# Global queries' scores: 128 weight columns instead of 32, and the global keys repeated behind the last key block

## The chip, the core and the metric

The kernel runs on one core of a Trainium2 chip. The metric is the time of one execution on the device in microseconds (us). Three runs of the kernel before took 1181.5, 1179.32 and 1181.81 us; their median is 1181.5 us.

## The reference, cut to what matters

```python
def _attn_ref(q_l, k_l, v_l, q_g, k_g, v_g):          # 8 batches, 8 heads, 512 local and 32 global tokens, 64 wide
    k_all = np.concatenate([k_g, k_l], axis=2)
    v_all = np.concatenate([v_g, v_l], axis=2)
    s_g = scale * np.matmul(q_g, k_all.transpose(0, 1, 3, 2))      # global queries see all 544 keys
    out_g = np.matmul(sm(s_g), v_all)
    s_ll = scale * np.matmul(q_l, k_l.transpose(0, 1, 3, 2))
    s_ll = np.where(mask, s_ll, -1000000000.0)                     # mask: abs(pos[:, None] - pos[None, :]) <= 32
    s_lg = scale * np.matmul(q_l, k_g.transpose(0, 1, 3, 2))
    s_l = np.concatenate([s_lg, s_ll], axis=-1)                    # local queries: 32 global keys and a window
    out_l = np.matmul(sm(s_l), np.concatenate([v_g, v_l], axis=2))
    return np.concatenate([out_g, out_l], axis=2)

def _moe_ref(x, w_gate, w_val, w_out):                # 4608 tokens, 512 wide, 1536 hidden
    gate = 1.0 / (1.0 + np.exp(-(x @ w_gate)))
    val = x @ w_val
    return (gate * val @ w_out).astype(np.float32)
```

The attention output, heads side by side, is the input x of the gated network. All data are float32.

## The kernel before, in words

**Layout.** For each batch and head the host writes one array with 64 rows (the width of a head): 256 local queries, then the extended keys, then the other 256 local queries, then the 32 global queries. The extended keys are four blocks of 160 columns behind 32 zero columns; block j holds 64 local keys, the 32 global keys, and the next 64 local keys. 32 zero columns end them, which makes 704 (`KEXT`). So the global keys already stand once in each block, between the two halves of its local keys.

**Two forms of attention.** Fifty-two heads take a split form: each float32 operand is cast to a rounded part (`qk_hi`, a cast on ScalarE, L197) and a remainder (`kl` and part of `qk_hi`, subtractions on GpSimd, L198 and L200), and each score product is made twice, once per part, over 128 rows. The first twelve heads (all of batch 0, whose 512 tokens are worked on in two half chunks, and four of batch 1) take a native float32 form over 64 rows, in which every such product is two passes in the trace.

**Attention of local queries** (`local_unit`): two query blocks at a time, L234 (scores into PSUM), L248 and L251 (softmax on VectorE and ScalarE), L254 to L218 (normalising into `p_buf`), L270 (transposes on TensorE), L281 and L282 (the transposed weights into SBUF as `pt`: a cast on ScalarE, then a subtraction on VectorE), L301 and L302 (products with the values), L304 to L306.

**Global queries** (`global_scores`, once per head). The weights of the product are the 32 global queries; the moving operand is the extended keys. One bank, `sa` (named `bank_x`), takes two products of 256 columns per part (L318): the first 64 columns of each of the four blocks, then the last 64 of each. A second bank, `sb` (named `bank_y`), takes the 32 global keys (L320). ScalarE copies both banks into 32 rows of `pg` (L322, L323). When four heads have filled the 128 rows, `global_group` makes the softmax over columns 0 to 543 and the products with the values.

**The gated network** (`ffn_stream`): for each chunk of 512 tokens and each of 12 tiles of the hidden width, 12 products of 512 columns for the gate (`bank_g`, L400), 12 for the value (`bank_v`, L400), and 12 of the output (`bank_o`, L437) for the tile before.

**What sets the order.** A queue of events with written due times places the attention's pieces between groups of four network products. A scheduler then orders each engine's instructions by priority and allots buffers. All attention banks and `bank_g` and `bank_v` share four PSUM buffers (tag `att`), so a product that opens a bank waits until the readers of the bank that had the buffer are done. In the first 160 us the network's weights are also loaded and converted: L137 and L141 on ScalarE, L139 and L140 on VectorE, L142 on GpSimd, loads by L126.

## Time and profile before

| | |
|---|---|
| median of 3 runs | 1181.5 us (1179.32 to 1181.81) |
| the profiled execution | 1179.81 us, of which the span from first to last instruction is 1177.9 us |
| TensorE products (PE) | busy 1146.4 us, 97% of the span |
| TensorE weight loads (PEld) | busy 962.3 us, 82% |
| VectorE (DVE), ScalarE (ACT), GpSimd (POOL) | 773.7 us, 753.2 us, 413.3 us |
| granted TensorE clock | 1.000 |

Products are pipelined: the duration of one includes its way through the array, so 0.28 us for 256 columns does not mean that the next one starts 0.28 us later. What a product costs its engine is the distance between starts, and that is read from the timeline. An idle time is printed behind the instruction that ended it, with the instruction it waited for.

### The profile page before, as it was taken

Reading aid. Unit: us, or ns where it says so; the run is one execution under the profiler, and the core shown is the slowest. Engines: PE = TensorE matmul, PEld = TensorE weight load, DVE = VectorE, ACT = ScalarE, POOL = GpSimd, SP = SyncE. Lnnn points to the kernel's source line nnn. Section 1 sums busy time; section 2 is a strip of 40 time slices with the busy share of each in tenths; the row PEclk is TensorE's granted clock in tenths of the full one; section 3 lists DMA queues with packets and bytes.
Section 4 is the critical chain, followed back from the end, with each engine's and each line's share of the span. In section 5 each row is a group of like instructions: output and inputs, shape, how many; then the busy total and the mean of one; then the engine's idle time right before and its main releaser. Section 6 shows DMA issues by size and latency. Waiting matters only on the chain.

```text
span 1177.9 us, 19115 instructions
## 1 busy us (share of the span) xinstructions
PE 1146.4 (97%) x6596; PEld 962.3 (82%) x6596; DVE 773.7 (66%) x2132; ACT 753.2 (64%) x1737; POOL 413.3 (35%) x408
## 2 busy tenths in 40 slices
PE   8999999999999999999999999999999999999998
PEld 7777788888888888888888888888888888888897
DVE  5677657577676677667676677667676677533343
ACT  5898877566675676666675676666675675532343
POOL 2444435334353444334352444334452443100000
PEclk9999999999999999999999999999999999999999
DMA  8888844333443343343343343343344342122143
GB/s 295 283 288 279 259 134 128 95 116 94 115 116 113 106 115 98 106 140 90 113 115 114 105 116 98 107 149 91 103 116 122 99 118 81 44 100 72 54 151 118
DMA packets 59489, 151.81 MB, mean 129 GB/s; under 512 B 6144, under 2 KB 19456, under 8 KB 59392
## 3 DMA queue, kind: packets, MB, share of 16 engines
q1 hardware_dynamic: 59392, 150.59, 42.2%
q8 instruction: 52, 0.85, 0.3%
q14 instruction: 45, 0.37, 0.1%
HBM read 135.36 MB, written 15.20 MB: 128 GB/s over the span
## 4 chain that ended last, share of the span: by engine, by line
PE 75%; DVE 11%; ACT 8%; issue 3%; DMA 2%; POOL 1%; SPq 0%; ACTq 0%; DVEq 0%; POOLq 0%
PE bank_v L400 20%; PE bank_g L400 19%; PE bank_o L437 19%; PE bank_x L234 4%; DVE p_buf L218 4%; PE bank_y L270 4%; ACT s_sb L251 3%; PE bank_x L301 2%; PE bank_x L302 2%; PE bank_x L318 2%; PE bank_x L361 1%; DVE bank_v L420 1%; DVE bank_v L421 1%; PE bank_o L110 1%; ACT hh L423 1%
## 5 line engine op out<-in xcount | busy, mean ns | idle before, releaser
L400 PE MATMUL bank_v<-xt,wv 128*128 128x512 f32 (+1 forms) x1440 | 328.3, 364 | 14.1 <-DVE pt L282 14.1
L400 PE MATMUL bank_g<-xt,wg 128*128 128x512 f32 (+1 forms) x1440 | 330.4, 364 | 0.1
L437 PE MATMUL bank_o<-wo,hh 128*128 128x512 f32 x1224 | 329.2, 400 | 1.2 <-ACT hh L423 1.2
L400 PEld LDWEIGHTS bank_v<-xt,wv 128*128 128x128 f32 x1440 | 237.1, 189 | 51.0 <-issue 16.0
L400 PEld LDWEIGHTS bank_g<-xt,wg 128*128 128x128 f32 x1440 | 236.8, 189 | 37.4 <-issue 2.5
L437 PEld LDWEIGHTS bank_o<-wo,hh 128*128 128x128 f32 x1224 | 217.2, 189 | 41.8 <-ACT hh L423 3.0
L251 ACT ACTIVATE s_sb<-s_sb,nm 128x192 f32<-128x192 f32 (+1 forms) x240 | 110.4, 462 | 98.2 <-DVE nm L248 97.3
L218 DVE TENSOR_SCALAR p_buf<-s_sb,r 128x128 f32<-128x128 f32 (+2 forms) x443 | 153.5, 383 | 6.6 <-PE bank_y L270 1.7
L306 POOL TENSOR_TENSOR x<-t 64x256 f32<-64x256 f32 x104 | 76.4, 735 | 172.1 <-DVE t L305 146.1
L211 POOL TENSOR_TENSOR vhl<-v_raw,vhl 128x512 fp32r<-128x512 f32 x52 | 67.2, 1293 | 187.4 <-ACT vhl L210 104.1
L198 POOL TENSOR_TENSOR kl<-qk_raw,qk_hi 128x704 fp32r<-128x704 f32 x52 | 88.6, 1703 | 108.3 <-ACT qk_hi L197 107.8
L423 ACT CAST hh<-bank_v 128x512 fp32r<-128x512 f32 (+1 forms) x120 | 62.7, 522 | 96.1 <-DVE bank_v L421 95.2
L408 ACT ACTIVATE th<-bank_g 128x512 f32<-128x512 f32 (+1 forms) x120 | 63.7, 531 | 87.0 <-PE bank_g L400 86.6
L413 DVE TENSOR_SCALAR mn<-bank_g 128x512 f32<-128x512 f32 (+1 forms) x108 | 67.4, 624 | 71.8 <-ACT th L408 71.8
L305 DVE TENSOR_TENSOR t<-bank_x,t 64x512 f32<-64x512 f32 x104 | 70.7, 680 | 62.0 <-ACT t L304 61.1
L420 DVE TENSOR_TENSOR bank_v<-bank_v,mn 128x512 f32<-128x512 f32 (+1 forms) x120 | 73.6, 614 | 53.5 <-PE bank_v L400 48.4
L248 DVE CUSTOM_DVE_ANT_0 s_sb<-bank_x,masks 128x192 f32<-128x192 f32 (+1 forms) x240 | 79.9, 370 | 38.5 <-PE bank_x L234 35.6
L424 DVE TENSOR_TENSOR hh<-bank_v,hh 128x512 fp32r<-128x512 f32 (+1 forms) x120 | 73.0, 608 | 35.1 <-ACT hh L423 33.2
L200 POOL TENSOR_TENSOR qk_hi<-qk_raw,qk_hi 64x256 fp32r<-64x256 f32 x104 | 80.3, 792 | 4.1
L421 DVE SCALAR_TENSOR_TENSOR bank_v<-th,bank_v 128x512 f32<-128x512 f32 (+1 forms) x120 | 73.2, 610 | 1.8
L414 ACT ACTIVATE mn<-mn 128x512 f32<-128x512 f32 (+1 forms) x108 | 62.9, 583 | 12.9 <-DVE mn L413 8.2
L270 PE MATMUL bank_y<-ident,p_buf 128*128 128x128 f32 x440 | 69.7, 274 | 1.3 <-ACT mn L410 0.5
(108 smaller groups left out, 1648.7 us busy)
## 6 DMA issues: line engine op xcount, KB each, us to landing
wo<-wo_dram SPq DMA_DIRECT2D x116, 512.0 KB, 3.4
qk_raw<-in_qk_dram SPq DMA_DIRECT2D x104, 312.0 KB, 4.4
v_raw<-in_v_dram SPq DMA_DIRECT2D x52, 256.0 KB, 2.6
out_dram<-ob SPq DMA_DIRECT2D x34, 256.0 KB, 2.9
xt<-in_w_gate_dram SPq DMA_DIRECT2D x12, 512.0 KB, 5.4
xt<-in_w_val_dram SPq DMA_DIRECT2D x12, 512.0 KB, 5.0
xt<-in_w_out_dram SPq DMA_DIRECT2D x12, 512.0 KB, 5.3
v_nat<-in_v_dram SPq DMA_DIRECT2D x8, 512.0 KB, 7.6
```

Source lines behind the costliest of these rows:

```text
L198: nc.gpsimd.tensor_tensor(kl, t[:, K0:Q1], hi[:, K0:Q1].bitcast(F32), op=ALU.subtract)
L200: nc.gpsimd.tensor_tensor(hi[64:128, r], t[64:128, r], hi[64:128, r].bitcast(F32), op=ALU.subtract)
L218: nc.vector.tensor_scalar(out, in_, by, None, op0=ALU.mult)
L248: anchor[0] = nc.vector.tensor_tensor_reduce(out=s_sb[:, i, w], in0=s_ps[:, i, w], in1=mid[:, w], scale=-0.125, scalar=3.0e38, op0=ALU.add ...
L251: exp_at[0] = nc.scalar.activation(s_sb[:, i, w], s_sb[:, i, w], AF.Exp, bias=nm[:, i:i + 1], scale=-1.0, accum_out=sm[:, i:i + 1])
L270: nc.tensor.transpose(pt_ps[:, t], flat[:, t * P:(t + 1) * P], ident)
L306: nc.gpsimd.tensor_tensor(dst, t0[:, :, 0], t0[:, :, 1], op=ALU.add)
L400: nc.tensor.matmul(acc, w[a][:, t, fs], xt[:, c, t, x0:x0 + ntok], start=n == 0, stop=n == 11)
L420: nc.vector.tensor_tensor(acc, acc, mn, op=ALU.mult)
L421: nc.vector.scalar_tensor_tensor(acc, th, 1.0, acc, op0=ALU.add, op1=ALU.mult)
L423: nc.scalar.copy(hh[:, 0, 0:ntok], acc)
L437: nc.tensor.matmul(o_ps[t], ph[:, a, t * P:(t + 1) * P], pwo[:, c], start=f2 == 0 and i == 0, stop=f2 == NF - 1 and i == 2)
```

## The change

The weights of the global scores become the last 128 query columns (96 local queries and then the 32 global ones), and only rows 96 to 127 of the result are used. The extended keys get 32 more columns: where 32 zero columns stood behind the fourth block now stand the 32 global keys once more, and 32 zero columns follow them. So one product of 5 x 64 = 320 columns covers the first halves of four blocks and the global keys, and one of 4 x 64 = 256 columns the last halves. Each takes a bank of its own, and ScalarE copies each into `pg` with one instruction. Columns 544 to 575 of `pg`, which were zero, are now written with the scores of the zero keys, which are zero.

```diff
-KEXT = 4 * BLK + 64
+KEXT = 4 * BLK + 3 * 32
     def global_scores(T, row):
         ks, k0s, q0 = T["qk"], T["k0"], T["q0"]
         last = len(ks) - 1
-        qg = ks[0][:, QK - SG - q0:QK - q0]
-        sa = ps.tile([SG, 4, P], F32, name="bank_x", tag="att", bufs=4)
-        sb = ps.tile([SG, SG], F32, name="bank_y", tag="att", bufs=4)
-        for half in range(2):
-            o0 = 96 * half
+        qg = ks[0][:, QK - P - q0:QK - q0]
+        rows = slice(SG * row, SG * (row + 1))
+        for half, n in enumerate((5, 4)):
+            sg = ps.tile([P, n, 64], F32, name="bank_x", tag="att", bufs=4)
             for t, (src, k0) in enumerate(zip(ks, k0s)):
-                view = src[:, k0 + 32:k0 + 32 + 4 * BLK].rearrange("p (j c) -> p j c", c=BLK)[:, :, o0:o0 + 64]
-                nc.tensor.matmul(sa[:, :, 64 * half:64 * half + 64], qg, view, start=t == 0, stop=t == last)
-        for t, (src, k0) in enumerate(zip(ks, k0s)):
-            nc.tensor.matmul(sb, qg, src[:, k0 + 96:k0 + 128], start=t == 0, stop=t == last)
-        rows = slice(SG * row, SG * (row + 1))
-        nc.scalar.copy(pg[rows, 0:SL], sa.rearrange("p a c -> p (a c)"))
-        nc.scalar.copy(pg[rows, SL:KALL], sb)
+                k = src[:, k0 + 32 + 96 * half:k0 + 96 + 96 * half]
+                view = bass.AP(k.tensor, k.offset, [k.ap[0], (BLK, n), (1, 64)])
+                nc.tensor.matmul(sg, qg, view, start=t == 0, stop=t == last)
+            nc.scalar.copy(pg[rows].rearrange("p (j c) -> p j c", c=P)[:, 0:n, 64 * half:64 * half + 64], sg[P - SG:])
...
     ke = np.zeros((N, KEXT, D), np.float32)
+    ke[:, 32 + 4 * BLK:64 + 4 * BLK] = kg
```

Line numbers behind `global_scores` fall by four (L400 becomes L396, L437 becomes L433, L408, L414 and L415 become L404, L410 and L411); both copies are L319.

The order on TensorE, at one of the twelve places where the value bank `bank_v` of the network follows a head's global scores. What each product waits for stands in brackets. Before:

```order
L400 MATMUL bank_g<-xt,wg_108 128x512 x4
L318 MATMUL bank_x<-qk_hi 32x4x64 [waits DVE_49]
L318 MATMUL bank_x<-kl,qk_hi 32x4x64
L318 MATMUL bank_x<-qk_hi 32x4x64
L318 MATMUL bank_x<-kl,qk_hi 32x4x64
L320 MATMUL bank_y<-qk_hi 32x32 [waits DVE_49]
L320 MATMUL bank_y<-kl,qk_hi 32x32
L400 MATMUL bank_v<-xt,wv_110 128x512 [waits DVE_49,PE_49]
```

And now:

```order
L396 MATMUL bank_g<-xt,wg_108 128x512 x4
L318 MATMUL bank_x<-qk_hi 128x320 [waits DVE_49]
L318 MATMUL bank_x<-kl,qk_hi 128x320
L318 MATMUL bank_x<-qk_hi 128x256 [waits DVE_49]
L318 MATMUL bank_x<-kl,qk_hi 128x256
L396 MATMUL bank_v<-xt,wv_110 128x512 [waits DVE_49,PE_49]
```

Six products become four; the wait for the second bank moves from behind four products to behind two; the wait of `bank_v` stands where it stood. Around the split heads' global scores this is the only change of TensorE's order.

The order on ScalarE at such a place, from the gate's `th` to the next transposed weights `pt`. Before:

```order
L408 ACTIVATE th<-bank_g 128x512
L322 COPY pg_buf<-bank_x 32x512
L415 ACTIVATE th<-th 128x512
L414 ACTIVATE mn<-mn 128x512
L323 COPY pg_buf<-bank_y 32x32
L304 COPY t_3431<-bank_x 64x512
L197 CAST qk_hi<-qk_raw 128x1248
L281 CAST pt<-bank_y 128x512
```

And now:

```order
L404 ACTIVATE th<-bank_g 128x512
L319 COPY pg_buf<-bank_x 32x5x64
L411 ACTIVATE th<-th 128x512
L319 COPY pg_buf<-bank_x 32x4x64
L410 ACTIVATE mn<-mn 128x512
L304 COPY t_3405<-bank_x 64x512
L197 CAST qk_hi<-qk_raw 128x1280
L281 CAST pt<-bank_y 128x512
```

The second copy has moved ahead of one activation, and the cast of the queries and keys has 32 more columns.

The order on ScalarE in the first 160 us, between two conversions of the output weights (`wo_hi`) and of the gate's (`wg`). Before:

```order
L141 CAST wo_hi<-xt 128x512
L137 ACTIVATE xt<-xt 128x512
L251 ACTIVATE s_sb,sm<-s_sb,nm 128x224
L251 ACTIVATE s_sb,sm<-s_sb,nm 128x192
L423 CAST hh<-bank_v 128x256
L297 COPY x_552<-bank_x 64x256
L216 ACTIVATE p_buf<-s_sb,r 128x96
L372 CAST xt<-x_552 128x256
L216 ACTIVATE p_buf<-s_sb,r 128x128
L322 COPY pg_buf<-bank_x 32x512
L323 COPY pg_buf<-bank_y 32x32
L141 CAST wg_108<-xt 128x4x128
```

And now:

```order
L141 CAST wo_hi<-xt 128x512
L419 CAST hh<-bank_v 128x256
L251 ACTIVATE s_sb,sm<-s_sb,nm 128x224
L251 ACTIVATE s_sb,sm<-s_sb,nm 128x192
L297 COPY x_551<-bank_x 64x256
L137 ACTIVATE xt<-xt 128x512
L368 CAST xt<-x_551 128x256
L216 ACTIVATE p_buf<-s_sb,r 128x96
L216 ACTIVATE p_buf<-s_sb,r 128x128
L319 COPY pg_buf<-bank_x 32x5x64
L319 COPY pg_buf<-bank_x 32x4x64
L278 COPY pt_nat<-bank_y 128x512
```

Conversions (L137, L141) have moved back by a few places behind attention and network work; such moves of one to four places run through ScalarE's and VectorE's order of the first 160 us.

## Rows read from the trace of the kernel before

**Rows 1.** The profile page: busy time by engine, and the chain of work that ended last by engine.

```profile
PE 1146.4 (97%) x6596; PEld 962.3 (82%) x6596; DVE 773.7 (66%) x2132; ACT 753.2 (64%) x1737; POOL 413.3 (35%) x408
...
PE 75%; DVE 11%; ACT 8%; issue 3%; DMA 2%; POOL 1%; SPq 0%; ACTq 0%; DVEq 0%; POOLq 0%
```

**Rows 2.** Busy time of each engine by stretch (us from the span's start, length, then PE, PEld, DVE, ACT and POOL busy with instruction counts, granted clock, DMA share, GB/s): a stretch of the start, and one batch of the steady part.

```profile
40.00:80.00 40.00, 38.65 (x265) 29.59 (x264) 26.83 (x80) 36.61 (x105) 14.15 (x12) 1.00 0.86 289
...
514.00:646.00 132.00, 129.65 (x717) 108.89 (x717) 93.31 (x258) 87.67 (x194) 54.67 (x54) 1.00 0.39 111
```

**Rows 3.** The table of waits of TensorE, its two longest lines (what waited, for what, us in total, times, longest).

```profile
PE bank_v L400 <- DVE pt L282: 14.1, 12, 1.2
PE bank_x L301 <- DVE pt L282: 3.9, 5, 1.4
```

**Rows 4.** The timeline of TensorE at a split head's global scores behind which TensorE does not wait (start, duration, engine, line, operation, count).

```profile
699.66 0.28 PE L318 MATMUL bank_x<-qk_hi 128*32 128x256 f32 x1
...
700.16 0.18 PE L320 MATMUL bank_y<-kl,qk_hi 128*32 128x32 f32 x1
700.20 1.17 PE L400 MATMUL bank_g<-xt,wg 128*128 128x512 f32 x4
701.20 0.28 PE L301 MATMUL bank_x<-pt,vhl 128*128 128x256 f32 x1
...
701.67 1.09 PE L400 MATMUL bank_g<-xt,wg 128*128 128x512 f32 x4
702.60 0.60 PE L270 MATMUL bank_y<-ident,p_buf 128*128 128x128 f32 x4
...
704.89 0.26 PE L234 MATMUL bank_x<-qk_hi 128*128 128x192 f32 x1
...
705.32 0.64 PE L400 MATMUL bank_v<-xt,wv 128*128 128x512 f32 x2
```

**Rows 5.** Weight loads by line and shape: busy us in all, mean ns of one.

```profile
L302 PEld LDWEIGHTS bank_x<-pt,vhl 128*128 128x128 f32 x208 | 39.2, 189 | 3.7
L318 PEld LDWEIGHTS bank_x<-qk_hi 128*32 128x32 f32 x104 | 11.2, 108 | 2.8
```

**Rows 6.** The timeline of all engines at one of the twelve places of the first line of rows 3.

```profile
270.61 1.94 DVE L218 TENSOR_SCALAR p_buf<-s_sb,r 128x96 f32<-128x96 f32 x4
...
271.33 0.28 PE L318 MATMUL bank_x<-qk_hi 128*32 128x256 f32 x1
...
271.83 0.18 PE L320 MATMUL bank_y<-kl,qk_hi 128*32 128x32 f32 x1
272.15 0.57 ACT L322 COPY pg_buf<-bank_x 32x512 f32<-32x512 f32 x1
272.47 0.54 DVE L282 TENSOR_TENSOR pt<-bank_y,pt 128x384 fp32r<-128x384 f32 x1
...
273.16 0.70 PE L400 MATMUL bank_v<-xt,wv 128*128 128x512 f32 x2 [1.15 <-DVE pt L282]
```

**Rows 7.** The timeline of all engines 0.8 us behind the start of global scores at the beginning of a batch.

```profile
375.34 0.56 DVE L282 TENSOR_TENSOR pt<-bank_y,pt 128x384 fp32r<-128x384 f32 x1 [0.45 <-ACT pt L281]
...
376.11 0.28 PE L301 MATMUL bank_x<-pt,vhl 128*128 128x256 f32 x1
```

**Rows 8.** The chain that ended last, in order of time, from the first split head with global scores on (start, us on the chain, what).

```profile
173.78 1.15 ACT qk_hi L197
...
174.99 1.72 POOL kl L198
...
186.97 0.36 PE bank_x L301
...
199.77 0.35 PE bank_x L301
```

**Rows 9.** The timeline of TensorE at a native head's global scores.

```profile
87.43 0.38 PE L294 MATMUL bank_x<-pt_nat,v_nat 128*64 128x128 f32 x2
87.74 0.86 PE L400 MATMUL bank_g<-xt,wg 128*128 128x256 f32 x5
88.53 1.05 PE L318 MATMUL bank_x<-qk_nat 64*32 64x256 f32 x4
89.42 0.22 PE L320 MATMUL bank_y<-qk_nat 64*32 64x32 f32 x2
89.57 0.86 PE L400 MATMUL bank_v<-xt,wv 128*128 128x256 f32 x5
```

**Rows 10.** Groups of instructions of ScalarE and GpSimd by shape: busy us in all, mean ns of one, idle before.

```profile
L322 ACT COPY pg_buf<-bank_x 32x512 f32<-32x512 f32 x64 | 36.7, 574 | 32.1 <-PE bank_y L320 31.5
...
L323 ACT COPY pg_buf<-bank_y 32x32 f32<-32x32 f32 x64 | 10.9, 171 | 0.3
...
L197 ACT CAST qk_hi<-qk_raw 128x1248 fp32r<-128x1248 f32 x52 | 64.2, 1235 | 0.6
...
L198 POOL TENSOR_TENSOR kl<-qk_raw,qk_hi 128x704 fp32r<-128x704 f32 x52 | 88.6, 1703 | 108.3 <-ACT qk_hi L197 107.8
...
L211 POOL TENSOR_TENSOR vhl<-v_raw,vhl 128x512 fp32r<-128x512 f32 x52 | 67.2, 1293 | 187.4 <-ACT vhl L210 104.1 <-issue 74.0 <-DMA qk_raw<-in_qk_dram 9.4
```

**Rows 11.** The chain that ended last, its longest pieces between 90 and 125 us.

```profile
97.34 6.46 DMA xt<-in_w_gate_dram
...
118.31 1.58 issue
```

## The prediction

> **What bounds the kernel now.** I read the page first: TensorE's products fill 97% of the span and make up 75% of the chain that ended last, with 11% on VectorE and 8% on ScalarE [rows 1]. In a batch of the steady part TensorE is busy 129.65 of 132 us, VectorE 93.31, ScalarE 87.67 [rows 2]. So what TensorE spends counts, unless a wait behind it takes it back. The table of waits names those: the value bank waits 12 times, 14.1 us in all, for VectorE's subtraction L282, and L301 waits five times, 3.9 us, for the same line [rows 3]. Third came the timeline, because a busy time says little of pipelined products: I read distances between starts.
>
> **What global scores cost now.** At a head without a wait, from the first score product to L301 pass 701.20 - 699.66 = 1.54 us [rows 4]: 0.54 us for the four products of 256 columns and the two of 32, then 1.00 us for four network products. Four network products behind products of 256 columns take 702.60 - 701.67 = 0.93 us. So 0.07 us lie behind the two short products. What could cause it: the next product's 128-column weights take 189 ns to load, and 32 columns of product don't cover that [rows 5].
>
> **What they cost then.** Products of 256 columns with 128-column weights stand 0.47 / 4 = 0.1175 us apart (701.20 to 701.67), those of 512 columns 0.2325 us. The trace has none of 320. Its bounds are these two; between them by columns it is 0.1175 + 64 x 0.00045 = 0.146 us, and I take that, for products are paid by columns in both. The head becomes 2 x 0.146 + 2 x 0.1175 + 0.93 = 1.457 us, 0.083 less; 1.54 and 0.93 are rounded to hundredths, and I use 0.085. At 0.1175 for the 320 it would be 0.14 less, at 0.2325 0.09 more.
>
> **Where that counts.** There are 52 split heads.
> - Twelve are the waits of rows 3. There the score products end at about 272.0, and the value bank starts at 273.16, 0.15 us behind L282's end, which stands in VectorE's queue behind four L218 begun at 270.61 [rows 6]. None of these reads a global score. TensorE arrives 0.01 us earlier and waits longer: 0.
> - The first four split heads run into L301's waits (three of the five in rows 3, and the chain before them). From 173.78 to 186.97 the chain is ScalarE, GpSimd and VectorE; TensorE is late only at its end, and again at 199.77 [rows 8]. Gain 0. But the cast L197 and the subtraction L198 on that chain get 32 more columns: 0.84 ns a column on ScalarE, from (574 - 171) / 480, makes 0.027 us, and 2.1 ns on GpSimd, from (1703 - 1293) / 192, makes 0.068 us. The second copy ahead of the cast grows from 32 to 256 columns, 0.19 us; the first shrinks by 192 columns, 0.16 us, and starts 0.18 us sooner, after two products. Between -0.05 and +0.29 us; I take +0.1.
> - Five heads at the beginning of a batch have L301 close behind: it starts 0.21 us after L282's end, against 0.15 where it waits, so 0.06 us can be won; one of the five in rows 3 is such a head and wins nothing [rows 6, 7]. Five times 0.03: 0.15 us.
> - The other 31 keep 0.085 us: 2.64 us.
>
> The second bank's wait, now behind two products instead of four, comes 0.18 us sooner; its readers are activations and subtractions of the units before, and rows 3 show no split head that waits there. If one did, it would cost up to 0.18 us, at a single head.
>
> **The twelve native heads.** From first score pass to the next network product pass 89.57 - 88.53 = 1.04 us [rows 9]. A pass of 256 columns is 0.89 / 4 = 0.22 us, so one of 320 is 0.28. Behind a native product the next network product comes late: two passes of 128 columns, 0.11 each, take 0.31 (87.43 to 87.74), 0.09 more. Then: 0.28 + 0.28 + 0.22 + 0.31 = 1.09 us, 0.05 more each, for now the long pass stands last instead of the short one. All twelve on the path would be +0.6 us; but in the start ScalarE is busy 36.61 of 40 us [rows 2] and much of the chain is there, so the floor is 0 and I take +0.1.
>
> **What is hidden.** The two copies go from 574 + 171 to about 413 + 359 ns [rows 10], 0.03 us more a head, and the cast 0.03. ScalarE has 44 idle us in 132 to cover it; without that cover it would be 52 x 0.06 = 3 us. The loads grow by 32 of 1248 columns, and in the steady part DMA is 39% busy [rows 2]. In the start it is 86%; there an order that has moved by a few places is worth perhaps 1.2 us either way (two instructions of about 0.6 us), and I take 0.
>
> **Sum.** -2.64 - 0.15 + 0.1 + 0.1 = -2.6 us. Against the profiled execution (1179.81) that is 1177.2 us. The median of the runs shown is 1181.5, so the profiled one was a quick one; from the mean of all four, 1180.6, I get 1178.0 us, and that is my forecast.
>
> **Weights of 128 columns against the trace.** A weight load goes from 108 to 189 ns [rows 5], and each of the four products has its own. In the trace products of 192 columns with such weights stand (705.32 - 704.89) / 4 = 0.1075 us apart, little less than those of 256 (0.1175) [rows 4]; so something of about 0.108 us bounds short products, and 256 and 320 columns lie above it. The Trainium skill, "TensorE: Matmul & The Clock Gate", section "LDWEIGHTS (loading the stationary operand)", says that a load takes its columns divided by 1.2 ns: an estimate of 27 ns for 32 columns and 107 for 128. The trace agrees with the difference (80 by that rule, 81 by rows 5), and 107 is near the 0.108. By that rule alone, were loads not hidden, four of them would cost 0.32 us a head.
>
> **The rivals.**
> 1. *The loads show.* If the larger loads are not hidden behind 320 and 256 columns, each costs up to 189 - 108 = 81 ns: 4 x 0.081 x 52 = 16.8 us, less 2.6: 1195 us. It decides from 13 ns a load (2.6 us / 208). Against it: the 0.1175 us of L301 and L302, which have those loads. This is the slower end; 4 in 100.
> 2. *The start slips.* Conversions of the network's weights stand later in ScalarE's order. The chain there holds one load of 6.46 us and a gap of 1.58 us [rows 11]: it is tight. A slip of one such gap is 1.6 us; two (3.2 us) undo the gain, 1181.2 us; from four on the kernel is slower, 1184.4 us. 4 in 100 for two, 7 for four. Against it: TensorE waits little there, 38.65 of 40 us busy.
> 3. *VectorE takes it back.* Every head's saving is waited off at the next bank that VectorE must release, as at the twelve: only the +0.2 remain, 1180.8 us. For it: 11% of the chain, and rows 7. Against it: 75% on TensorE. 16 in 100.
> 4. *More is kept.* The twelve heads keep theirs too, since L282 comes sooner as well: 43 x 0.085 and the 0.15, 1176.9 us. 10 in 100.
> 5. *The twelve waits go.* 14.1 us more: 1164 us. VectorE's order around L282 is unchanged, so 3 in 100.
>
> **Chances.** The forecast has 56 in 100, with a spread of 1.2 us from the start (1176.8 to 1179.2 us). A measurement of this kernel tells about 0.2%, 2.4 us, from no change, and -2.6 lies just beyond: six tenths of the forecast's chance, 34, are faster, 22 within. Faster: 34 + 10 + 3 = 47. Within: 22 + 16 + 4 = 42. Slower: 4 + 7 = 11. The range, 1174 to 1182.5 us, holds the forecast, rivals 3 and 4, two slips, and the 320 at either cost up to half its way to the bounds; the runs before already lie 2.5 us apart.
>
> **What would show it.** In the profile after: score products of 320 columns 0.146 us before the next start, 256 at 0.1175; four network products behind them in 0.93 instead of 1.00 us, and L301 1.46 us behind the first score product. The twelve waits for L282 stay at 14 us or grow by 0.01 each. Weight loads of L318 read 189 ns. At the native heads 1.09 us to the network's next product. I am wrong if L301 follows in 1.54 us or more, if L301's waits grow past five, or if the first 173 us change by more than 1.2 us.

## The result, and the profile after

Four runs of the changed kernel took 1194.6, 1191.26, 1193.86 and 1190.27 us, median 1192.56. The kernel before, run beside it, has a median of 1181.47 us. The ratio is 1.0104, with a 95% interval from 1.0090 to 1.0118: the change makes the kernel about 12 us slower. The forecast was 1178.0 us and its range ended at 1182.5, so the sign was wrong as well as the size. The profiled execution, the longest of the four, took 1194.6 us, 1192.4 of it from first to last instruction.

The page of the changed kernel: busy time by engine, the granted clock in 40 slices, the chain by engine.

```profile
PE 1155.6 (97%) x6468; PEld 969.5 (81%) x6468; DVE 777.9 (65%) x2132; ACT 760.5 (64%) x1737; POOL 418.4 (35%) x408
...
PEclk9998989999999999999999999999999999999999
...
PE 72%; DVE 10%; ACT 6%; issue 2%; POOL 1%; DMA 0%; SPq 0%; ACTq 0%; DVEq 0%
```

Against [rows 1] TensorE has 128 products fewer and is busy 9 us longer. The fourth and sixth slices (89 to 119 and 149 to 179 us) read 8 where the clock stood at full speed before.

Two stretches of the start that [rows 2] do not hold, of the kernel before (stretch, length, busy PE, PEld, DVE, ACT, POOL, clock, DMA share, GB/s):

```profile
80.00:120.00 40.00, 38.76 (x262) 29.99 (x260) 31.51 (x85) 35.61 (x98) 17.54 (x15) 1.00 0.88 283
120.00:160.00 40.00, 38.82 (x250) 31.24 (x250) 25.95 (x76) 32.38 (x88) 18.03 (x14) 1.00 0.71 222
```

The same view of the changed kernel: the three stretches of the start, and the batch that answers to the one in [rows 2], 12.3 us later.

```profile
40.00:80.00 40.00, 38.22 (x244) 29.05 (x243) 26.05 (x76) 36.30 (x101) 13.41 (x11) 1.00 0.84 276
80.00:120.00 40.00, 35.53 (x222) 27.37 (x221) 27.65 (x71) 30.65 (x82) 16.04 (x13) 0.91 0.78 255
120.00:160.00 40.00, 36.98 (x213) 29.03 (x211) 27.24 (x69) 30.84 (x81) 16.32 (x12) 0.91 0.70 219
...
526.30:658.30 132.00, 129.41 (x697) 108.72 (x696) 93.34 (x258) 87.88 (x191) 54.86 (x54) 1.00 0.39 112
```

In the last two stretches of the start TensorE is busy 3.2 and 1.8 us less than before, runs at 0.91 of its clock, and ScalarE is busy 5.0 and 1.5 us less. In the batch nothing looks lost, and nothing won.

**The split heads did as forecast.** The timeline of TensorE of the changed kernel, at the head that answers to [rows 4]:

```profile
712.40 0.32 PE L318 MATMUL bank_x<-qk_hi 128*128 128x320 f32 x1
712.55 0.31 PE L318 MATMUL bank_x<-kl,qk_hi 128*128 128x320 f32 x1
712.70 0.28 PE L318 MATMUL bank_x<-qk_hi 128*128 128x256 f32 x1
712.82 0.28 PE L318 MATMUL bank_x<-kl,qk_hi 128*128 128x256 f32 x1
712.93 1.10 PE L396 MATMUL bank_g<-xt,wg 128*128 128x512 f32 x4
713.87 0.28 PE L301 MATMUL bank_x<-pt,vhl 128*128 128x256 f32 x1
```

Products of 320 columns start 0.15 us before the next, those of 256 0.12; four network products take 0.94 us, and L301 follows in 1.47 us (forecast 0.146, 0.1175, 0.93, 1.46). Over the heads without a wait, 40 before and 39 after, score products and first network product take 849 ns before and 769 after at the median.

**Weight loads, copies, cast and subtraction** of the changed kernel, by shape (busy us in all, mean ns), which answer to [rows 5, 10]:

```profile
L198 POOL TENSOR_TENSOR kl<-qk_raw,qk_hi 128x736 fp32r<-128x736 f32 x52 | 92.2, 1774 | 109.7 <-ACT qk_hi L197 106.4 <-PE bank_x L294 2.8
...
L197 ACT CAST qk_hi<-qk_raw 128x1280 fp32r<-128x1280 f32 x52 | 65.6, 1262 | 0.6
...
L319 ACT COPY pg_buf<-bank_x 32x320 f32<-32x320 f32 x64 | 26.9, 420 | 28.8 <-PE bank_x L318 28.0
...
L319 ACT COPY pg_buf<-bank_x 32x256 f32<-32x256 f32 x64 | 23.3, 363 | 0.8 <-PE bank_x L318 0.4
...
L318 PEld LDWEIGHTS bank_x<-qk_hi 128*128 128x128 f32 x104 | 19.5, 188 | 2.5 <-DVE mn L409 0.3
```

All five are within 7 ns of their working in the prediction.

**The waits of TensorE** in the changed kernel, whole execution:

```profile
PE bank_v L396 <- DVE pt L282: 13.9, 12, 1.2
PE bank_x L301 <- DVE pt L282: 3.9, 5, 1.2
...
PE bank_x L318 <- DVE mn L409: 3.0, 1, 3.0
PE bank_y L270 <- DVE hh L420: 2.0, 1, 2.0
```

The first two lines are those of [rows 3], all but unmoved. The last two are new, and both lie in the start. Here is the larger one, at the eleventh native head (timeline of TensorE and VectorE):

```profile
145.50 1.30 DVE L140 SCALAR_TENSOR_TENSOR xt<-xt 128x512 uint32<-128x512 uint32 x1 [0.32 <-ACT xt L137]
145.63 0.80 PE L318 MATMUL bank_x<-qk_nat 64*128 64x320 f32 x2
146.72 0.41 DVE L139 TENSOR_SCALAR xt<-xt 128x512 uint32<-128x512 uint32 x1
...
147.52 1.55 DVE L218 TENSOR_SCALAR p_buf<-s_sb,r 128x128 f32<-128x128 f32 x2
148.99 0.41 DVE L409 TENSOR_SCALAR mn<-bank_g 128x256 f32<-128x256 f32 x1
...
149.46 1.22 PE L318 MATMUL bank_x<-qk_nat 64*128 64x256 f32 x2 [3.02 <-DVE mn L409]
```

The second score bank takes the buffer of a gate bank, whose last reader L409 stands in VectorE's queue behind two conversions of the network's weights (L140, L139) and the normalising L218. So TensorE stands still behind two passes of 320 columns. Before, the 32 global keys waited there too, but for 0.6 us and behind four passes (timeline of TensorE and VectorE of the kernel before):

```profile
138.15 1.05 PE L318 MATMUL bank_x<-qk_nat 64*32 64x256 f32 x4
...
139.35 0.40 DVE L413 TENSOR_SCALAR mn<-bank_g 128x256 f32<-128x256 f32 x1
139.67 0.28 DVE L218 TENSOR_SCALAR p_buf<-s_sb,r 128x128 f32<-128x128 f32 x1
...
139.81 0.25 PE L320 MATMUL bank_y<-qk_nat 64*32 64x32 f32 x2 [0.61 <-DVE mn L413]
```

There the gate's reader (L413, now L409) stands ahead of the L218, in the changed kernel behind them. Two passes of 320 columns end only about 0.25 us sooner than the four passes of before; so most of the longer wait comes from this order on VectorE.

**The clock.** The next view is busy time by stretch, behind the two new waits (same columns as above):

```profile
108.00:112.00 4.00, 2.01 (x15) 1.80 (x14) 3.83 (x12) 3.40 (x12) 1.54 (x1) 0.93 0.97 316
112.00:116.00 4.00, 4.00 (x9) 2.13 (x8) 2.54 (x9) 2.37 (x8) 0.00 (x0) 0.50 0.96 353
116.00:120.00 4.00, 4.00 (x23) 3.15 (x22) 2.00 (x3) 2.57 (x7) 2.51 (x2) 0.72 0.44 154
...
144.00:148.00 4.00, 2.44 (x17) 1.80 (x15) 3.54 (x11) 3.31 (x9) 1.77 (x2) 1.00 0.96 318
148.00:152.00 4.00, 2.54 (x8) 1.64 (x8) 3.20 (x7) 2.69 (x8) 1.98 (x2) 0.62 0.67 208
152.00:156.00 4.00, 4.00 (x12) 2.56 (x12) 0.00 (x0) 1.65 (x4) 1.37 (x2) 0.53 0.27 100
```

Twice TensorE is busy for little more than half of 4 us, and then the clock stands at half speed. Added up from the clock column, the three stretches from 108 us lose 3.4 us of full speed (0.07, 0.50 and 0.28 of 4 us), and the last two 3.4 us (0.38 and 0.47). With the two new waits (2.0 and 3.0 us) that is an estimate of 11.8 us, nearly all of the 12.3 us that the start loses (next table). The native head at 112.79 us runs its passes in 695, 533, 427 and 561 ns, where others of the same execution take 373, 269, 216 and 306. The times of the four runs go with the clock: those with a granted clock of 0.994 took 1194.6 and 1193.86 us, those with 0.997 took 1191.26 and 1190.27. The Trainium skill, "TensorE: Matmul & The Clock Gate", section "What's actually happening", says that TensorE is set to half rate after an idle window of about 3.4 us. Here TensorE was not idle that long: the waits were 2.0 and 3.0 us, and the stretches of 4 us ahead of the half clock were half busy.

**Where the 14.5 us between the two profiled executions lie.** I set the start of each of the 4104 network products beside its start before (us later than before). The table holds most runs of the next section as well; network product 0 starts at 36.1 us before, 396 at 160.5, where the start is over, 3384 at 1039.7, where attention is over, and 3744 at 1121.4, towards the end of the pure network.

| kernel | 0 | 108 | 216 | 288 | 324 | 396 | 3384 | 3744 | last |
|---|---|---|---|---|---|---|---|---|---|
| changed kernel | -0.3 | 3.0 | 7.2 | 7.5 | 12.2 | 12.3 | 12.8 | 14.4 | 14.5 |
| e1 split heads only | 0.0 | 0.0 | 0.5 | 0.9 | 2.9 | 2.9 | 3.1 | 4.7 | 4.8 |
| e2 native heads only | -1.2 | 2.2 | 4.7 | 5.5 | 8.1 | 8.2 | 10.5 | 12.1 | 12.2 |
| e3 keys only | 0.0 | 0.0 | 1.2 | 1.5 | 3.4 | 3.4 | 9.6 | 11.2 | 11.3 |
| e5 before, moved | -0.7 | -0.7 | -0.7 | -0.8 | 1.8 | 1.8 | 5.0 | 6.6 | 6.7 |
| e6 changed, moved | -1.1 | 2.3 | 4.8 | 5.3 | 8.4 | 8.5 | 7.2 | 7.2 | 7.2 |
| e7 in place, split | 0.1 | 0.2 | 0.4 | 0.4 | 0.4 | 0.4 | 12.4 | 12.4 | 12.4 |
| e8 in place, all | 0.2 | 3.9 | 3.2 | 4.0 | 6.4 | 6.7 | 18.9 | 18.9 | 18.9 |
| e9 in place, zeroed | -0.9 | -0.9 | -1.5 | -1.2 | 1.2 | 1.2 | -2.2 | -2.2 | -2.2 |
| e10 before, aligned | -0.9 | -0.6 | -0.7 | -0.7 | 1.4 | 1.4 | 1.0 | 1.0 | 1.1 |
| e11 e9, aligned | -0.7 | -0.7 | -0.7 | -0.7 | -0.7 | -0.7 | -4.4 | -4.4 | -4.4 |
| e13 native wide | 0.0 | 0.5 | 0.7 | 0.9 | 2.1 | 2.6 | 3.9 | 3.9 | 3.9 |
| e14 two banks | -1.3 | 2.6 | 6.0 | 6.8 | 11.0 | 11.0 | 11.3 | 11.3 | 11.4 |
| e15 before, off 128 | -0.2 | -0.2 | 1.3 | 1.3 | 3.0 | 3.0 | 4.1 | 4.1 | 4.1 |
| e16 conversions later | -0.3 | -0.4 | 0.3 | 0.5 | 3.2 | 3.2 | 3.3 | 3.3 | 3.3 |
| e17 e1, moved | 0.2 | 0.1 | 0.9 | 1.3 | 3.3 | 3.3 | 1.1 | 1.1 | 1.1 |

The column of product 396 needs care. The kernel before was profiled in an execution whose clock was 1.00 from 120 to 160 us. e5, e9, e10, e13 and e15 keep its order (e9, and e11 below, add a few short instructions on VectorE), and the same stretch of their traces has 0.96; they are 1.2 to 3.0 us late. e7 and e11, with its order and 1.00, are 0.4 late and 0.7 early. So 1 to 3 us of a lag there can belong to the execution and not to the kernel.

The changed kernel loses 12.3 us in the start, wins nothing where the split heads are, and loses 1.6 us in the pure network, where not one instruction differs. There the reading is plain. TensorE's timeline of the kernel before (start, duration, line, count):

```profile
1061.42 2.88 PE L400 MATMUL bank_g<-xt,wg 128*128 128x512 f32 x12
1064.14 2.88 PE L400 MATMUL bank_v<-xt,wv 128*128 128x512 f32 x12
1066.86 2.88 PE L437 MATMUL bank_o<-wo,hh 128*128 128x512 f32 x12
1069.58 2.88 PE L400 MATMUL bank_g<-xt,wg 128*128 128x512 f32 x12
```

and of the changed kernel:

```profile
1074.65 2.95 PE L396 MATMUL bank_g<-xt,wg 128*128 128x512 f32 x12
1077.44 2.96 PE L396 MATMUL bank_v<-xt,wv 128*128 128x512 f32 x12
1080.23 2.90 PE L433 MATMUL bank_o<-wo,hh 128*128 128x512 f32 x12
1082.97 2.95 PE L396 MATMUL bank_g<-xt,wg 128*128 128x512 f32 x12
```

Twelve products take 2.72 us before; twelve of the gate or the value take 2.79 now. No engine is waited for. The 320 products from 3420 to 3740 take 73.07 us before and 74.49 now.

### The profile page after: what moved, and what is told of

Its sections match the earlier page's. It is cut to its first block, busy times and chain, and to the rows that moved or that the text cites. A ratio compares the mean times of both kernels' runs of the same rounds, so it can differ in the third digit from the quotient of the medians.

```text
span 1192.4 us, 18863 instructions
## 1 busy us (share of the span) xinstructions
PE 1155.6 (97%) x6468; PEld 969.5 (81%) x6468; DVE 777.9 (65%) x2132; ACT 760.5 (64%) x1737; POOL 418.4 (35%) x408
## 4 chain that ended last, share of the span: by engine, by line
PE 72%; DVE 10%; ACT 6%; issue 2%; POOL 1%; DMA 0%; SPq 0%; ACTq 0%; DVEq 0%
PE bank_v L396 20%; PE bank_g L396 19%; PE bank_o L433 19%; DVE p_buf L218 4%; PE bank_y L270 3%; PE bank_x L234 3%; ACT s_sb L251 2%; PE bank_x L318 2%; PE bank_x L301 2%; PE bank_x L302 2%; PE bank_x L357 1%; DVE bank_v L416 1%; DVE t L305 1%; DVE bank_v L417 1%; DVE mn L409 1%
## 5 line engine op out<-in xcount | busy, mean ns | idle before, releaser
L396 PE MATMUL bank_v<-xt,wv 128*128 128x512 f32 (+1 forms) x1440 | 330.9, 366 | 14.0 <-DVE pt L282 13.9
L396 PE MATMUL bank_g<-xt,wg 128*128 128x512 f32 (+1 forms) x1440 | 331.6, 365 | 0.1
L433 PE MATMUL bank_o<-wo,hh 128*128 128x512 f32 x1224 | 329.5, 401 | 1.6 <-ACT hh L419 1.5
L396 PEld LDWEIGHTS bank_v<-xt,wv 128*128 128x128 f32 x1440 | 237.5, 189 | 55.8 <-issue 18.4
L396 PEld LDWEIGHTS bank_g<-xt,wg 128*128 128x128 f32 x1440 | 237.3, 189 | 39.3 <-issue 2.8
L433 PEld LDWEIGHTS bank_o<-wo,hh 128*128 128x128 f32 x1224 | 219.2, 190 | 44.3 <-issue 3.9
L218 DVE TENSOR_SCALAR p_buf<-s_sb,r 128x128 f32<-128x128 f32 (+2 forms) x443 | 153.5, 383 | 6.7 <-PE bank_y L270 1.7
L198 POOL TENSOR_TENSOR kl<-qk_raw,qk_hi 128x736 fp32r<-128x736 f32 x52 | 92.2, 1774 | 109.7 <-ACT qk_hi L197 106.4
L404 ACT ACTIVATE th<-bank_g 128x512 f32<-128x512 f32 (+1 forms) x120 | 63.9, 532 | 86.4 <-PE bank_g L396 86.0
L409 DVE TENSOR_SCALAR mn<-bank_g 128x512 f32<-128x512 f32 (+1 forms) x108 | 67.4, 624 | 72.8 <-ACT th L404 72.8
L270 PE MATMUL bank_y<-ident,p_buf 128*128 128x128 f32 x440 | 69.6, 274 | 2.6 <-DVE hh L420 2.0
L410 ACT ACTIVATE mn<-mn 128x512 f32<-128x512 f32 (+1 forms) x108 | 62.9, 582 | 12.5 <-DVE mn L409 7.2
```

The lines of the kernel that those rows point to most:

```text
L198: nc.gpsimd.tensor_tensor(kl, t[:, K0:Q1], hi[:, K0:Q1].bitcast(F32), op=ALU.subtract)
L218: nc.vector.tensor_scalar(out, in_, by, None, op0=ALU.mult)
L270: nc.tensor.transpose(pt_ps[:, t], flat[:, t * P:(t + 1) * P], ident)
L396: nc.tensor.matmul(acc, w[a][:, t, fs], xt[:, c, t, x0:x0 + ntok], start=n == 0, stop=n == 11)
L409: nc.vector.tensor_scalar(mn, acc, 0.0, None, op0=ALU.min)
L433: nc.tensor.matmul(o_ps[t], ph[:, a, t * P:(t + 1) * P], pwo[:, c], start=f2 == 0 and i == 0, stop=f2 == NF - 1 and i == 2)
```

## The experiments

Ratios are to the kernel before, run on the same chip, with their 95% intervals. In words, theory A: the native heads' new form upsets the start. B: the wide weights cost time in the split heads. C: the 32 more key columns upset the start.

### One part of the change at a time (e1 to e4)

e1, the changed kernel with the old form in the native heads:

```diff
+    def global_scores(T, row):
+        (scores_old if T["native"] else scores_new)(T, row)
```

> The new products for the 52 split heads alone; the twelve native heads keep the six old products (both read the keys with 32 more columns). Theory A (the loss is made in the first 160 us, because the native heads' new products change the order that the scheduler gives the conversions of the weights and the four shared banks; the products themselves are as cheap as predicted): 1179 to 1182 us, network product 324 starts within 2 us of where it does before (143.4 us). Theory B (the 128 weight columns cost time in the split heads): about 1190 us, with the lag growing evenly between 180 and 1040 us. Theory C (the 32 more key columns, through loads and casts, upset the start): about 1190 us, product 324 late by 8 us or more.

Measured: 1185.96 us, 1.0049 (1.0034 to 1.0064), above A's range. No half clock, and 2.9 us late at product 396.

e2, the other way round (`scores_new if T["native"] else scores_old`):

> The new products for the twelve native heads alone; the split heads keep the six old ones. Theory A: as the changed kernel, 1191 to 1195 us, product 324 late by about 12 us, all lost before 160 us. Theory B: about 1183 us. Theory C: as the changed kernel, but no more than e3 with the keys alone.

Measured: 1194.76 us, 1.0124 (1.0102 to 1.0146). Product 324 is 8.1 us late, where A had about 12, and 4.0 us more are lost behind the start, where A had nothing.

e3, `KEXT` and the host's line `ke[:, 32 + 4 * BLK:64 + 4 * BLK] = kg` alone:

> Only the 32 more key columns (and the global keys written there, which nobody reads); all heads keep the six old products. Theory A: 1180 to 1183 us, nothing lost in the start but a few tenths. Theory B: 1181 us, as before. Theory C: about 1190 us, product 324 late by 8 us or more.

Measured: 1188.89 us, 1.0073 (1.0055 to 1.0090), though no product has changed.

e4, the changed kernel with narrow weights:

```diff
-        qg = ks[0][:, QK - P - q0:QK - q0]
+        qg = ks[0][:, QK - SG - q0:QK - q0]
...
-            sg = ps.tile([P, n, 64], F32, name="bank_x", tag="att", bufs=4)
+            sg = ps.tile([SG, n, 64], F32, name="bank_x", tag="att", bufs=4)
...
-            nc.scalar.copy(pg[rows].rearrange("p (j c) -> p j c", c=P)[:, 0:n, 64 * half:64 * half + 64], sg[P - SG:])
+            nc.scalar.copy(pg[rows].rearrange("p (j c) -> p j c", c=P)[:, 0:n, 64 * half:64 * half + 64], sg)
```

> The changed kernel with 32 weight columns in place of 128: the order on all engines is that of the changed kernel. Theory A: 1190 to 1194 us, the loss stays, since order and banks are the changed kernel's. Theory B: 1178 to 1181 us, the loss goes with the wide weights. Theory C: 1190 to 1194 us. If the wide weights matter at all, the native products should start closer together here (269 ns or less where the changed kernel's trace shows 373, 269, 216 and 306).

Measured: 1190.09 us, 1.0085 (1.0061 to 1.0109). Of the native passes only the first comes closer to the next, 293 ns in place of 373. In split heads without a wait, score products and first network product take 764 ns, where the changed kernel has 769.

B is out: narrow weights keep most of the loss, and e1 is below e3 by the 2.4 thousandths (2.8 us) that the split heads were to save. Theory A holds for the difference between e1 and the changed kernel (1.0104 - 1.0049). But no theory had e3: 3.4 us of its lag arise in the start, and 6.2 us between 160 and 1040 us, where A and C expected nothing. Of these 6.2 us, 3.0 are lost at one place of its trace, at 511 us, where VectorE waits 2.9 us for an output store and TensorE behind it; the rest grows evenly. The pure network was slower in all four by the same 1.6 us. What the four share are 32 more key columns, and these make five buffers (`qk_raw`, two `qk_hi`, two `kl`) 128 bytes longer each, so that xt, hh and wo stand 640 bytes further on. In the built programs' tables of buffers they and the network's weights wg and wv begin at multiples of 256 bytes before; in the changed kernel xt, hh and wo are 128 bytes off.

### Addresses (e5, e6, e15, e10, e12)

e5 moves buffers in the kernel before and changes nothing else; every engine's order is the same.

```diff
+    gap = ctx.enter_context(tc.tile_pool(name="gap", bufs=1))
+    gap.tile([P, 160], F32, name="gap")
```

> The kernel before with 640 unused bytes per partition behind its attention buffers, so that the network's operands (xt, hh, wo) stand where they stand in the changed kernel; the order on all engines is that of before. Theory D (the address alone sets the network products' pace: about 232.5 ns where before's trace has 226.7 in the pure network behind 1020 us): the 320 products from 3420 to 3740 take 74.5 us in place of 73.1, the share of products slower than 227.9 ns between 1020 and 1080 us is over 0.7, and the time is 2 to 5 us above before. Theory E (the pace is a state of one execution or of one chip): 73.1 us and no difference, or either by chance.

Measured: 1185.53 us, 1.0043 (1.0026 to 1.0059). The timeline in the pure network of e5:

```profile
1066.84 2.95 PE L402 MATMUL bank_g<-xt,wg 128*128 128x512 f32 x12
1069.63 2.96 PE L402 MATMUL bank_v<-xt,wv 128*128 128x512 f32 x12
1072.43 2.90 PE L439 MATMUL bank_o<-wo,hh 128*128 128x512 f32 x12
```

It is the changed kernel's pace, in the kernel before: 640 unused bytes cost about 5 us (3.1 to 7.0), 3.2 of it in the trace between products 396 and 3384 and 1.6 in the pure network.

e6, the changed kernel with the same lines and `[P, 32]`, 128 bytes:

> The changed kernel with 128 unused bytes per partition, so that xt, hh and wo begin at multiples of 256 bytes again, as before; same order as the changed kernel. Theory D in the form that 256 bytes are what matters: the 320 products from 3420 to 3740 take 73.1 us, and the time is 2 to 4 us below the changed kernel (about 1188 to 1190 where that is 1192.5). If only the old addresses do, or theory E: 74.5 us and 1192 us.

Measured: 1187.53 us, 1.0059 (1.0039 to 1.0079), and the timeline of e6 has the old pace:

```profile
1068.59 2.88 PE L398 MATMUL bank_g<-xt,wg 128*128 128x512 f32 x12
1071.31 2.88 PE L398 MATMUL bank_v<-xt,wv 128*128 128x512 f32 x12
```

Whether the moving operand's address counts, or how the two operands stand to each other, e15 asks: 128 unused bytes ahead of `ident` in the kernel before, so that the weights wg and wv move as well.

> The kernel before with all buffers from ident on moved by 128 bytes, the network's weights (wg, wv) too; same order. Theory G (a network product is slow where its two operands differ by 128 bytes modulo 256): 73.1 us for the 320 products from 3420 to 3740, 1179 to 1183 us. Theory H (it is slow where the moving operand xt begins 128 bytes off a multiple of 256, whatever the weights): 74.5 us, 1183 to 1187 us.

Measured: 1180.9 us, 1.0001 (0.9984 to 1.0017), and 73.07 us for the 320 products. So theory G stands: a network product is slow where its two operands differ by 128 bytes modulo 256. It fits that eight of the twelve `bank_o` products of the changed kernel keep 227 ns, for hh and wo have moved together; why the other four are slow it does not say.

In the kernel before most network products between attention's are slow as well (54% to 78% of them over 227.9 ns in stretches of 60 us from 240 to 1020 us, with a mean of 230 to 232). From the fourth one behind the transposes L270, whose operand `ident` is 128 bytes off, it is 82%, behind the scores L234 none. e10 puts every operand of TensorE of the kernel before on a multiple of 256 bytes, with unused columns:

> The kernel before, with unused bytes between its buffers so that every operand of TensorE (ident, masks, queries, keys, values, pt, x32, xt, hh, wo) begins at a multiple of 256 bytes; same order on all engines. Theory F (behind a product whose operand begins 128 bytes off, the network's products go on at about 232 ns instead of 226.7): the share of network products slower than 227.9 ns between 180 and 1040 us falls from 0.5 to 0.8 to under 0.2, the spacing's mean from 231 to 227, and the time by 8 to 14 us, to 1167 to 1173 us. Rival (the transposes themselves slow what follows, whatever the address of ident): shares as before, 1179 to 1183 us.

Measured: 1178.85 us, 0.9985 (0.9971 to 0.9999), with 72% slow products from 300 to 360 us (76% before) and 82% behind L270. Theory F fell: what follows L270 is slow wherever `ident` stands. In e10 48% of those from the fourth on behind the scores are slow too, where it was none. So the transposes need not be the cause, and it stays open.

e12, the changed kernel aligned in the same way:

> The changed kernel with every operand of TensorE at a multiple of 256 bytes; same order as the changed kernel. Theory F with A: the network's pace is e10's, and what is left between the two is the changed kernel's start (8 to 12 us lost before 160 us) less what its split heads save (2 to 3 us): 5 to 10 us above e10, 1173 to 1181 us. If the addresses also made the start's loss: within 2 us of e10.

Measured: 1185.66 us, 1.0060 (1.0034 to 1.0085), as e6. The start's loss of 8.4 us stays.

### The start's order kept, and the key columns in place (e7, e8, e9, e11)

The old keys ended in 32 zero columns that nobody reads. e7 puts the global keys there, so that loads and casts stay as they were; the fifth piece of 64 columns then takes 32 columns that are no keys, whose scores must not count.

```diff
-        kl = spl.tile([P, KEXT], F32R, name="kl")
+        kl = spl.tile([P, KEXT + 32], F32R, name="kl")
...
-                nc.tensor.matmul(o_ps[:, r], pt[:, j, r].rearrange("p c q -> p (c q)"), T["v"][:, tiles[j], :],
+                kp = slice(0, SG if j == 4 else P)
+                nc.tensor.matmul(o_ps[:, r], pt[kp, j, r].rearrange("p c q -> p (c q)"), T["v"][kp, tiles[j], :],
...
+    ke[:, 32 + 4 * BLK:64 + 4 * BLK] = kg
```

> The global keys written into the 32 zero columns that stood behind the fourth block, no more columns loaded or cast (the subtraction of the key remainders is 32 columns longer), the new products for the split heads alone, and the products of the fifth tile of keys with the values over 32 rows. The start's order is that of before on every engine. Theory A (the changed kernel's loss lies in the start and in the network's pace, and its split heads save what was predicted): 1176 to 1179.5 us, below before; product 396 within 1 us of before. Theory B (the new products cost time in the split heads): above before, 1182 us or more.

Measured: 1193.99 us, 1.0113 (1.0094 to 1.0132), far off. The table shows where: 0.4 us late at product 396, so the start is sound, and then 12.0 us are lost up to product 3384, in steps of about 1 us, one for each group of four heads. The groups of e7's products with the values, by shape, say by what:

```profile
L379 PE MATMUL bank_x<-vhl,ptg 128*64 128x128 f32 x208 | 22.9, 232 | 0.0
...
L379 PE MATMUL bank_x<-vhl,ptg 32*64 32x128 f32 x52 | 14.0, 269 | 0.0
```

My 32-row products stand among 128-row ones; the twenty of a group take 2.27 us from first start to the next product, 1.19 before. 13 groups make 14 us. The Trainium skill, "TensorEngine Tiling (Array Packing)", section "Key Properties", says that a change of the tiling mode drains TensorE. The starts go with that, but do not show a drain: at the median 153 ns lie before each 32-row product and 199 and 111 behind it, in place of 60.

e8, the same with the new form for the native heads too:

> As e7, with the new products for the native heads too; no load has changed, so that the start's order moves only by the native heads' two new banks and copies. Theory A: product 396 is late by 7 to 10 us, with stretches of half clock between 100 and 160 us, and the time is 1186 to 1190 us. Theory C (it was the longer loads and casts that upset the start): as e7, 1176 to 1180 us.

Measured: 1198.75 us, 1.0146 (1.0124 to 1.0167), with product 396 late by 6.7 us, 6.3 more than in e7, though no load has changed. By the medians of e8 and e7 it is 4.8 us, and the clock, 0.96 from 120 to 160 us here and 1.00 in e7, has a part in the difference. That is for A, just below what I expected of product 396, and against C; the time missed both ranges because of the 32-row products. The wait of L318 for L411 is there (1.9 us), behind the same order on VectorE as in the changed kernel; that of L270, 2.0 us in the changed kernel, is not.

e9 goes back to 128 rows and zeroes the 32 columns of `pg` instead:

```diff
         p = pg[:, 0:KALL]
+        nc.vector.memset(pg[:, KALL:KALL + 32], 0.0)
```

> As e7, but the products of the fifth tile of keys go over 128 rows again, and VectorE sets the 32 unwanted columns of pg to zero once per group of four heads (16 short instructions). If e7 lost its 1.0 us per batch to the 32-row products, that is gone, and what the split heads save is left: network product 3204 starts 2 to 3 us before where it does in the kernel before, and the time is 1176 to 1179 us (0.2 to 0.4% below before). If e7 lost it to the new score products themselves (theory B): 1190 us or more, as e7.

Measured: 1178.0 us, 0.9983 (0.9968 to 0.9998). That is 2.0 us less than the kernel before (0.2 to 3.8). From product 396 on e9 gains 3.4 us on it; its heads without a wait take 763 ns in place of 849.

e11, e9 with every operand on a multiple of 256 bytes:

> e9 and e10 together. Theory F with A: e10's time less 2 to 4 us, 1164 to 1171 us. If the slow pace had hidden the new products' saving or made it: as e10 within 1 us.

Measured: 1177.97 us, 0.9978 (0.9963 to 0.9993). Theory F's range is missed. e11 is within 1 us of e10, as the second half of the expectation said, but the saving is there: its heads take 769 ns in place of e10's 848, and between products 396 and 3384 it gains 3.7 us where e10 gains about 0.3. Both e9 and e11 beat the kernel before and the changed one; between e9, e10 and e11 the times tell nothing.

### What in the native heads upsets the start (e13, e14, e16)

e13, only the wide weights, in the native heads of the kernel before (`qg` of 128 columns, rows 96 to 127 copied); the order is that of before:

> The kernel before with 128 weight columns for the global scores of the twelve native heads, and nothing else: six products, banks, loads and the order on all engines are those of before. If the wide weights are what the native heads lose by: product 396 is late by 5 us or more, 1185 us or above. If it is the order and the second bank (theory A): product 396 within 2.5 us of before, 1179 to 1183 us; the native products start a few tens of ns further apart, about 0.1 us per head.

Measured: 1182.02 us beside 1181.36 for the kernel before, 0.9989 (0.9968 to 1.0011), 2.6 us late at product 396. The native passes show the loads: 320 ns for the first and 203 for the last where it was 240 and 123.

e14, narrow weights and old products, but two full banks:

```diff
+        sa = ps.tile([SG, 4, 64], F32, name="bank_x", tag="att", bufs=4)
+        sb = ps.tile([SG, 5, 64], F32, name="bank_y", tag="att", bufs=4)
```

> The kernel before with 32 weight columns and the old product sizes, but in the native heads the scores stand in two banks as in the changed kernel (first halves of the blocks in one, last halves and global keys in the other), copied by three instructions. Theory A (two full banks move the start's order and add a wait for the second bank): product 396 is late by 4 to 9 us, 1184 to 1190 us. If two banks alone cost nothing: within 2.5 us at product 396, 1179 to 1183 us.

Measured: 1190.06 us, 1.0083 (1.0054 to 1.0111). Product 396 is 11.0 us late, more than the 4 to 9 expected, and the new wait is there, in e14's timeline of TensorE:

```profile
145.08 0.62 PE L334 MATMUL bank_x<-qk_nat 64*32 64x256 f32 x2
149.29 0.62 PE L334 MATMUL bank_y<-qk_nat 64*32 64x256 f32 x2 [3.60 <-DVE mn L432]
```

e16 moves the order of the start and no product: the first argument of `CONVERT` is -1 in place of -2.

> The kernel before with the conversions of the network's weights due one group of four products later (the first argument of CONVERT -1 in place of -2): nothing is computed otherwise, but in the first 160 us the scheduler's order moves about as much as by the change (47 instructions on VectorE, 50 on ScalarE, 24 on SyncE). Theory A (the start is set by the order of the conversions): product 396 is late by 3 us or more, 1183 us or above. If the order alone is harmless: within 2.5 us, 1179 to 1183 us.

Measured: 1183.61 us, 1.0021 (1.0007 to 1.0034), 3.2 us late at product 396. By the letter that just passes A's bound, but the clock is 0.96 from 120 to 160 us as in e5 and e15, whose order is that of before and whose lag is 1.8 and 3.0 us. By the times, this order costs 2.5 us (0.8 to 4.0), less than the 6 to 11 us of the two banks. It is another order than theirs, so it does not clear order as such.

### Do the causes add up (e17)

e17 is e1 with e6's 128 bytes.

> e1 (new products in the split heads alone, 32 more key columns) with 128 unused bytes, so that xt, hh and wo begin at multiples of 256 bytes; order as e1. If the causes add up: e1's 1.0049 less the 0.0044 that e5 and e6 show for the addresses, so 1.000 to 1.001 times before (1180 to 1183 us), the 320 products from 3420 to 3740 in 73.1 us, and between product 396 and the end about 3 us gained on before after a start 2 to 4 us late. If something else is in it: 1184 us or more.

Measured: 1180.97 us, 1.0006 (0.9990 to 1.0022), with 73.07 us for the 320 products, as expected.

In thousandths of the time before: addresses 4.4 (e5 has 4.3, the changed kernel less e6 4.5); the native heads' new form 5.5 (the changed kernel less e1; e6 less e17 is 5.3); longer loads and casts 3.0 (e3 less e5); the split heads -2.4 (e1 less e3). That is 10.5, and 10.4 was measured. In us: 5.2 + 6.5 + 3.5 - 2.8 = 12.4. Each term carries an uncertainty of about 2 us, as the intervals show.

The steps from the kernel before over e5, e3 and e1 to the changed kernel must add up, whatever the causes are, so the sum is no proof. Runs outside these steps test it: e17 has 0.6 where e1 less the addresses gives 0.5, and e2 has 12.4 where addresses, loads and native heads give 12.9. For the native heads alone e8 less e7 has 3.3, without the wait of L270, and e14 has 8.3, with three copies in place of two; their size is known less well than the rest.

Runs that were granted the full clock (1.000) scatter less. Their means, less those of the kernel before beside them, are 5.2 us for e5, 8.9 for e3, 6.1 for e1, 0.8 for e17, -2.7 for e9, -0.9 for e10 and -3.4 for e11 (two to eight runs each). That is 5.2 us again for the addresses, 3.7 for the loads, and 2.8 won by the split heads (2.5 from e10 to e11).

## Why the prediction was wrong

**Right: the split heads.** The 31 heads at 0.085 us each were the sum's main term (2.64 us); heads without a wait save 0.080 (changed kernel) to 0.086 us (e9), and the runs give 2.8 us in all. The 320-column product at 0.146, the network products behind it, the twelve waits that stay at 14 us, copies and cast: all as worked out. Rival 1, the loads, is out for the split heads.

**Wrong: "In the start ... an order that has moved by a few places is worth perhaps 1.2 us either way ..., and I take 0."** The start lost 12.3 us in the profiled execution, so the prediction's own sign of being wrong (a change of more than 1.2 us in the first 173) came true. Two things were missed in that step. First, the size: another moved order cost 2.5 us (e16, 0.8 to 4.0), and the longer loads and casts, with the order they move, about 3.5 us. Second, it spoke of the conversions only. The bank wait was weighed for the split heads ("rows 3 show no split head that waits there") and not for the native ones, in whose stretch the four shared banks are contended: there the second bank, 0.6 us before, waited 3.0 us in the changed kernel, 1.9 in e8 and 3.6 in e14, because its buffer's last reader came later on VectorE, and the clock fell to half behind such waits. Rival 2 named the right place and direction with 7 in 100 for 1184.4 us, but by slips of conversions, which are a part of it.

**Wrong by a smaller amount: the native heads, "0.05 more each".** They take 1.164 us against the 1.04 of [rows 9], 0.125 more. The first pass of 320 columns takes 373 ns where I had 280. e13 shows the same with old columns, 80 ns more at the first and at the last pass, which is the difference of the loads in [rows 5] (189 - 108). In the new form e4 shows 80 ns of the 125, all at the first pass. So at the native heads rival 1 is right, for about 1 us in all, of which e13's time shows nothing.

**Not there at all: the addresses.** No step of the prediction asked what else stands behind a buffer that grows. 128 bytes more in each of five buffers cost about 5 us in network products that the change does not touch, as much as the native heads. It is why the gain of the split heads cannot be seen in the steady part of the changed kernel: between products 396 and 3384 it loses 0.5 us, and e6, with the operands moved back, gains 1.3, e17 2.2.

**Open.** Waits and clock together account for the start's loss: the two new waits and what the granted clock took add up to 11.8 us in the changed kernel, and in the same way to 7.6, 11.9, 7.8 and 8.0 in e2, e4, e6 and e12, which are 8.2, 11.5, 8.5 and 8.4 us late at product 396. What is not parted is how much the second bank costs without the order on VectorE that came with it: the order alone was tried only in e16, and no kernel had two full banks with the old order. How long the clock is halved differs between executions (6.8 us lost in the changed kernel's trace, 3.4 in e6's, with the same order), so a single trace tells the start's loss to no better than 3 us. Why network products between attention's are slow even with every operand aligned was not found, and offsets smaller than 128 bytes weren't tried.

## What to carry to other kernels

Before a buffer is made longer, list what stands behind it and keep its address modulo 256 bytes, or at least that of both operands of the main products together; the proof is a stretch of pure main work in both traces, where the same twelve products must take the same time. A change that fills or needs a bank of a contended pool in another way is priced at the place where the pool is tightest, not where most of its instances are, and there by the order of the engine that must release the bank. Where a stretch is tight on all engines, take the change out of that stretch and keep it where it pays: the split heads alone, with no load changed, gave 2.0 us (0.2 to 3.8) of the 2.6 that the whole change was to bring.

## What the runs showed of the hardware that I had not expected

- Two operands of a 512-column product whose addresses differ by 128 bytes modulo 256: 2.79 us for twelve products in place of 2.72 (232.5 against 226.7 ns each), with no wait shown anywhere (e5, e6, e15).
- A 32-row product among 128-row ones: 153 ns before it, 199 and 111 behind it, where 128-row neighbours stand about 60 ns apart (e7).
- Half clock after a stretch of 4 us in which TensorE was busy 2.0 to 2.4 us, though the waits there were 2.0 and 3.0 us; worth some 3 us between runs of the same kernel (1194.2 us on average at 0.994, 1190.8 at 0.997).
